# The second mixture's smallest expert in a round of 128 rows, with the rows as the stationary operand

## The chip, the core and the metric

The kernel runs on one core of a Trainium2 chip. Five engines work side by side, each with its own queue of instructions: TensorE (PE: products into PSUM banks; PEld is its loading of the stationary operand), VectorE (DVE), ScalarE (ACT), GpSimd (POOL) and SyncE (SP), which here issues the plain loads. The metric is the device time of one execution, in microseconds; lower is better.

## What is computed

A linear recurrence over 768 steps (its output is `x`, 3,072 tokens of 384 numbers), a first mixture of eight experts with 384 tokens each, and a second mixture, with which this case is concerned:

```python
def _moe2_ref(x, w_skip, w_gate, w1, w2):      # w1 [8, 384, 1024], w2 [8, 1024, 384]
    do_compute = x @ w_skip > 0
    out = x.copy()
    xc = x[do_compute]
    logits = xc @ w_gate
    e_idx = np.argmax(logits, axis=1)
    ...
    for e in range(E):
        mask = e_idx == e
        h = np.maximum(xc[mask] @ w1[e], 0.0)
        y[mask] = gate_w[mask, None] * (h @ w2[e])
    out[do_compute] = xc + y
```

How many tokens an expert of the second mixture gets follows from the data.

## The kernel before, in words

The kernel sorts the tokens of the second mixture by expert: each expert has 384 slots in a scratch tensor `xs2`, and the rows of its tokens are scattered there as the first mixture yields them. Slots without a token carry a row number out of bounds, so that the scatter of results passes over them.

The experts are taken by descending number of rows. `pick` finds the first, before the last tokens are known; its first 256 rows (`EARLY`) are computed while those arrive, and its next 128 (`LATE`) after. `ranks` sorts the other seven into rounds r = 1 to 7. The table `WIDE` says how many rows a round computes: 384 in round 1 and 256 in rounds 2 to 7 (entry 0 isn't used by the rounds). `ranks` also writes `room`, the number of rows that each expert's rounds cover; `rounds_more` compares it with the counts, and `moe2_more` runs further rounds over all experts if any count is larger. Whether it runs is told by `rest`, which every engine reads at the end, and SyncE already in the middle, ahead of the loads of round 1.

Products are made in three passes over float32 values split in two parts (`hi` and `lo`), which ScalarE (L976) and VectorE or POOL (L977) split from the loaded weights `raw`. Loads of weights have four `raw` buffers and the split ones twelve.

- `layer1` (L1018 on): for each of 8 blocks f of the hidden layer, 9 products `psh<-xT,hi` or `psh<-xT,lo` with the weights stationary and the rows moving, as many columns as the round has rows. ScalarE takes the relu (L1031), VectorE the difference (L1032).
- `layer1_few` (L1038 on), used so far for the first expert's 128 late rows: the rows are stationary and two blocks of weights (256 columns) move: `psh<-hi,xT`, 9 products for each of 4 groups. ScalarE takes the relu into `hr` (L1060), PE turns it (`pht<-ident,hr`, L112), ScalarE copies it (L1047) and VectorE makes the difference (L1048).
- `layer2` in `ffn2_out`: for each block of 128 rows, 8 x 3 products `psy<-...,hT` of 384 columns; then one output step on VectorE (`o<-psy`, L1223) and one scatter on POOL (L116).
- `prep2` issues the loads of the next round: the four weights of layer 1, the rows (`rows2`, L1174), the four of layer 2. `turn2` casts the row numbers (`ids`, L1202), turns the rows on PE (`pst<-ident,xg`, L112) and splits them (L985, L986).

`rows2` fills a tile with two buffers (`xg2`) for rounds of 256 rows or more, and a tile with one (`xl`) for 128. From the end of the first mixture on, a scheduler sets the order on each engine; loads wait in SyncE's queue until the buffer that they fill is free.

Of the kernel before, what the change touches and what calls it, by code (L numbers as in the profile page):

```python
# [8 lines left out]
F32 = mybir.dt.float32  # L9
# [5 lines left out]
ALU = mybir.AluOpType  # L15
# [16 lines left out]
def kernel_body(ctx, tc, q, k, v, a_re, a_im, w_gate, w1, w2, w_skip2, w_gate2, w12, w22, out):  # L32
    nc = tc.nc
    V = nc.vector
    B, H, S, D = q.shape
    DM = H * D
    E, _, F = w1.shape
# [5 lines left out]
    CAP = N // E  # L43


    ES = CAP
    WIDE = (CAP, CAP) + (256,) * (E - 2)
    MORE = 256

    EARLY, LATE = 256, 128  # L50
# [57 lines left out]
    def mat(*a, **kw):  # L108
        return pe(nc.tensor.matmul(*a, **kw))  # L109

    def tp(*a):
        return pe(nc.tensor.transpose(*a))  # L112
# [576 lines left out]
    room = rs.tile([128, E], F32, name="room")  # L689
# [5 lines left out]
    rw = ctx.enter_context(tc.tile_pool(name="rw", bufs=1))  # L695
# [322 lines left out]
    def layer1(w1h, xT, nt, tick=lambda: None, before=None, third=False):  # L1018
        hT = [fw.tile([128, KF, nt], F32R, tag=f"hT{i}", name="hT") for i in range(2)]
        for f in range(KF):  # L1020
            g, ff = divmod(f, FG)
            ps = pq.tile([128, nt], F32, tag="sm", name="psh") if third and f % 3 == 2 else pm.tile([128, nt], F32, tag="mm", name="psh")
            n = 0
            for a, b in PASSES:
                for c in range(KD):
                    mat(ps, lhsT=w1h[g][a][:, c, ff * 128:ff * 128 + 128], rhs=xT[b][:, c, :],
                       start=(n == 0), stop=(n == 3 * KD - 1))
                    n += 1
                    if n in (5, 9):
                        tick()  # L1030
            nc.scalar.activation(out=hT[0][:, f, :], in_=ps, func=ACTF.Relu)  # L1031
            V.scalar_tensor_tensor(out=hT[1][:, f, :], in0=ps, scalar=0.0, in1=hT[0][:, f, :].bitcast(F32),  # L1032
                                   op0=ALU.max, op1=ALU.subtract)
            if before:
                next(before, None)
        return hT

    def layer1_few(w1h, xT):  # L1038

        hT = [fw.tile([128, KF, 128], F32R, tag=f"hT{i}", name="hT") for i in range(2)]  # L1040

        def turned(g, h):
            pt = pt_.tile([128, FG, 128], F32, tag="t", name="pht")
            for f in range(FG):
                tp(pt[:, f, :], h[:, f * 128:(f + 1) * 128], ident)
            gs = slice(g * FG, (g + 1) * FG)
            nc.scalar.copy(out=hT[0][:, gs, :], in_=pt)  # L1047
            V.tensor_tensor(out=hT[1][:, gs, :], in0=pt, in1=hT[0][:, gs, :].bitcast(F32), op=ALU.subtract)  # L1048

        for g in range(NG):  # L1050
            ps = pm.tile([128, FG * 128], F32, tag="mm", name="psh")
            n = 0
            for a, b in PASSES:
                for c in range(KD):
                    mat(ps, lhsT=xT[b][:, c, :], rhs=w1h[g][a][:, c, :], start=(n == 0), stop=(n == 3 * KD - 1))
                    n += 1
            if g:
                turned(g - 1, h)
            h = rw.tile([128, FG * 128], F32, tag="R", name="hr", bufs=2)
            nc.scalar.activation(out=h, in_=ps, func=ACTF.Relu)  # L1060
        turned(NG - 1, h)
        return hT
# [48 lines left out]
    def route2(p, l2):  # L1111
# [37 lines left out]
        if p == E - 1:  # L1149
            ranks()  # L1150
# [16 lines left out]
    def by_load(r):  # L1167
        return ords[0:1, r:r + 1]

    def rows2(src, nj):  # L1170
        xg = fw.tile([128, nj, ROW], F32, tag="xg2", name="xg2", bufs=2) if nj > 1 else fw.tile([128, nj, ROW], F32, tag="xg", name="xl")

        def load_rows():
            nc.sync.dma_start(out=xg, in_=src)  # L1174
        return xg, load_rows

    def prep2(e, cap, shared, first=lambda: None):

        GF = FG * 128
        nj = cap // 128  # L1180
        if isinstance(e, int):
            er = slice(e, e + 1)
        else:
            er = nc.sync.value_load(e, min_val=0, max_val=E - 1)
            er = bass.ds(er, 1)
        xg, rows = rows2(xs2.rearrange("(e s) r -> e s r", e=E)[er, 0:cap, :].rearrange("o (j p) r -> p (o j) r", p=128), nj)
        w = weights(
            lambda g: w12[er, :, g * GF:(g + 1) * GF].rearrange("o (c p) f -> p (o c) f", p=128),
            lambda g: w22[er, g * GF:(g + 1) * GF, :].rearrange("o (c p) f -> p (o c) f", p=128), shared, {0: first, NG: rows})(2 * NG)
        return w, xg  # L1190

    def turn2(xg, res=None):
        res = [None] if res is None else res
        for _ in turn2_steps(xg, res):
            pass
        return res[0]
# [18 lines left out]
    def ffn2_out(xg, ids, w2h, hT, aside=True):  # L1215
        nj = xg.shape[1]
        pss = layer2(nj, 128, DM,
                     lambda f, a, b, j: hT[a][:, f, j * 128:(j + 1) * 128],
                     lambda f, a, b, j: w2h[f // FG][b][:, f % FG, :], aside=aside)
        o3 = fw.tile([128, nj, DM], F32, tag="yo", name="o3")  # L1220
        for j in range(nj):
            ot = o3[:, j, :]
            V.scalar_tensor_tensor(out=ot, in0=pss[j], scalar=xg[:, j, DM:DM + 1], in1=xg[:, j, 0:DM], op0=ALU.mult, op1=ALU.add)  # L1223
            scatter("out", out, ids[:, j:j + 1], ot, N - 1)
# [78 lines left out]
    def mixtures(exact, then=lambda: None):  # L1303
        (((w1h, w2h), xg), (ids, xT), last) = moe1(exact)
        hT = layer1(w1h, xT, EARLY, before=last)
        for _ in last:
            pass
        turn[1] = False
        res = then()
        er = nc.sync.value_load(head[0:1, 1:2], min_val=0, max_val=E * ES - LATE)  # L1310
        xl, load_rows = rows2(xs2[bass.ds(er, LATE), :].rearrange("(j p) r -> p j r", p=128), LATE // 128)
        nxt = prep2(by_load(1), WIDE[1], (2, 6), load_rows)
        ffn2_out(xg, ids, w2h, hT)
        ids, xT = turn2(xl)
        hT = layer1_few(w1h, xT)
        moe2_round(WIDE, by_load, 1, nxt, lambda: ffn2_out(xl, ids, w2h, hT))
        return res

    def moe2_round(caps, which, start=0, nxt=None, before=lambda: None):
        nxt = nxt or prep2(which(0), caps[0], (0, 1, 2))  # L1320
        cur = nxt + turn2(nxt[1])
        before()
        for r in range(start, E):
            (w1h, w2h), xg, ids, xT = cur
            hT = layer1(w1h, xT, caps[r], third=True)
            if r + 1 < E:
                nxt = prep2(which(r + 1), caps[r + 1], (2, 6))
                cur = nxt + turn2(nxt[1])
            ffn2_out(xg, ids, w2h, hT, aside=r + 1 < E)

    def ranks():

        sh = [128, E, E]
        kv = rw.tile([128, E], F32, tag="kv", name="kv")
        V.scalar_tensor_tensor(out=kv, in0=base2, scalar=float(E), in1=rev, op0=ALU.mult, op1=ALU.add)
        V.scalar_tensor_tensor(out=kv, in0=isfirst, scalar=FAR, in1=kv, op0=ALU.mult, op1=ALU.add)
        gt = rw.tile(sh, F32, tag="gt", name="gt")
        V.tensor_tensor(out=gt, in0=kv[:, None, :].to_broadcast(sh), in1=kv[:, :, None].to_broadcast(sh), op=ALU.is_gt)
        at_ = rw.tile([128, E], F32, tag="at_", name="at_")
        V.tensor_reduce(out=at_, in_=gt, axis=AX.X, op=ALU.add)  # L1340
        V.tensor_tensor(out=gt, in0=at_[:, None, :].to_broadcast(sh), in1=i128[:, 0:E, None].to_broadcast(sh), op=ALU.is_equal)
        V.tensor_tensor(out=gt, in0=gt, in1=rev[:, None, :].to_broadcast(sh), op=ALU.mult)
        V.tensor_reduce(out=kv, in_=gt, axis=AX.X, op=ALU.add)
        V.tensor_scalar(ords, kv, -1.0, float(E), op0=ALU.mult, op1=ALU.add)
        V.tensor_scalar(room, at_, float(WIDE.count(CAP)), float(CAP - MORE), op0=ALU.is_lt, op1=ALU.mult)
        V.tensor_scalar(room, room, float(MORE), None, op0=ALU.add)
        gap = rw.tile([128, E], F32, tag="gap", name="gap")
        V.tensor_scalar(gap, isfirst, float(EARLY), None, op0=ALU.mult)
        V.tensor_tensor(out=room, in0=room, in1=gap, op=ALU.subtract)
        V.scalar_tensor_tensor(out=room, in0=isfirst, scalar=ahead, in1=room, op0=ALU.mult, op1=ALU.add)  # L1350
# [99 lines left out]
```

## Time and profile before

| | us |
|---|---|
| median of 3 runs (lowest, highest) | 827.35 (827.09, 831.43) |
| the profiled execution | 826.72 |
| its span, first to last instruction | 824.8 |
| PE busy in the span | 705.2 (85%) |
| VectorE, ScalarE, POOL busy | 540.6, 389.0, 269.4 |
| mean granted clock of PE | 0.92 |

Times in the rows below count from the start of the span. "Idle before" an instruction, in square brackets, is followed by what ended it. A granted clock of 1.00 is full speed (2.4 GHz), 0.50 is 1.2 GHz. A busy time of PE includes the time in which products overlap, so the distance between the starts of two products is what one of them costs in a dense stretch.

### The profile page before, as it was taken

The numbers are of one execution on the slowest core, as the hardware profiler recorded it, in microseconds if no ns is written. First come the engines' busy times: TensorE is split into PE (matmuls) and PEld (weight loads), VectorE is DVE, ScalarE is ACT, GpSimd is POOL, SyncE is SP. The second block draws the span as 40 slices with busy tenths as digits, with TensorE's granted clock in tenths as the row PEclk, the third lists the DMA queues.
The fourth block names the chain that finished last, engine by engine and source line by source line (L and its number), as shares of the span: only waits on it lengthen the run. The fifth ranks groups of instructions, "written<-read, shape, count | busy, mean of one in ns | idle before, by whom it ended". The sixth has DMA issues, their size and how long they took to land.

```text
span 824.8 us, 14760 instructions
## 1 busy us (share of the span) xinstructions
PE 705.2 (85%) x5428; PEld 646.9 (78%) x5428; DVE 540.6 (66%) x1468; ACT 389.0 (47%) x682; POOL 269.4 (33%) x190
## 2 busy tenths in 40 slices
PE   1579879889999963888898898999999989999992
PEld 1468778788989952767787777898999979999992
DVE  8849789788756468789686787875534454544440
ACT  5775678667744313235151333343534255554530
POOL 1000545535501002010404041244214476776630
PEclk9669899999999975879997998999999989999996
DMA  9999565852411005144241515174206265566600
GB/s 171 175 293 164 76 129 108 131 110 64 72 41 40 20 31 181 45 138 147 65 136 53 177 37 175 33 228 135 72 16 201 87 212 192 193 210 227 226 27 12
DMA packets 183969, 100.03 MB, mean 121 GB/s; under 512 B 130963, under 2 KB 181129, under 8 KB 183888
## 3 DMA queue, kind: packets, MB, share of 16 engines
q1 hardware_dynamic: 178128, 86.99, 42.5%
q0 software_dynamic: 5760, 12.02, 4.3%
q8 instruction: 44, 0.72, 0.4%
q14 instruction: 37, 0.30, 0.1%
HBM read 82.23 MB, written 22.46 MB: 127 GB/s over the span
## 4 chain that ended last, share of the span: by engine, by line
PE 51%; DVE 18%; issue 9%; ACT 8%; DMA 8%; POOL 2%; SPq 2%; another core or an unknown queue 0%; DVEq 0%; POOLq 0%; ACTq 0%
PE psy L109 13%; PE psh L109 13%; DMA raw<-in_moe_w_dram 5%; PE py L109 4%; PE px L109 4%; PE pt L112 3%; DVE lo L977 3%; PE pa L109 3%; PE f L432 3%; PE st L109 2%; PE hist L109 2%; ACT hi L976 2%; DVE R L825 1%; DMA re<-in_a_re_dram 1%; DVE hT L1032 1%
## 5 line engine op out<-in xcount | busy, mean ns | idle before, releaser
L976 ACT CAST hi<-raw 128x768 fp32r<-128x768 f32 x128 | 107.0, 837 | 123.9 <-DMA raw<-in_moe_w_dram 92.0
L109 PE MATMUL psh<-xT,hi 128*128 128x384 f32 (+1 forms) x768 | 152.0, 330 | 6.9 <-DVE hT L1032 6.0
L109 PEld LDWEIGHTS psh<-xT,hi 128*128 128x128 f32 x768 | 124.1, 194 | 11.3 <-DVE hT L1032 8.3
L977 DVE TENSOR_TENSOR lo<-raw,hi 128x768 fp32r<-128x768 f32 x82 | 85.9, 1056 | 33.6 <-ACT hi L976 26.8
L109 PE MATMUL psy<-hT,hi 128*128 128x384 f32 x384 | 103.0, 350 | 0.0
L1031 ACT ACTIVATE hT<-psh 128x384 fp32r<-128x384 f32 (+1 forms) x128 | 56.0, 443 | 94.5 <-PE psh L109 89.0
L1032 DVE SCALAR_TENSOR_TENSOR hT<-psh,hT 128x384 fp32r<-128x384 f32 (+1 forms) x128 | 62.3, 492 | 53.6 <-ACT hT L1031 46.9
L977 POOL TENSOR_TENSOR lo<-raw,hi 128x768 fp32r<-128x768 f32 x46 | 85.4, 1875 | 33.5 <-ACT hi L976 22.8
L1002 POOL DMA_INDIRECT xg<-xd,ids x24 | 31.9, 1329 | 173.1 <-PE pp L109 62.4
L109 PE MATMUL psh<-xT,lo 128*128 128x384 f32 (+1 forms) x384 | 81.3, 321 | 0.0
L109 PE MATMUL psy<-hi,hT 128*128 128x384 f32 x288 | 79.3, 346 | 1.3 <-issue 1.3
L109 PEld LDWEIGHTS psy<-hT,hi 128*128 128x128 f32 x384 | 70.9, 194 | 0.6
L109 PE MATMUL psy<-hT,lo 128*128 128x384 f32 x192 | 68.9, 359 | 0.0
L109 PEld LDWEIGHTS psh<-xT,lo 128*128 128x128 f32 x384 | 65.3, 196 | 0.0
L109 PE MATMUL pa<-qT,kT 96*128 96x128 f32 x384 | 52.9, 284 | 1.7 <-ACT kT L497 1.7
L109 PEld LDWEIGHTS psy<-hi,hT 128*128 128x128 f32 x288 | 51.8, 192 | 1.8 <-issue 1.6
L116 POOL DMA_INDIRECT xs<-x,ix x24 | 25.0, 1043 | 80.2 <-issue 48.9
L109 PEld LDWEIGHTS pa<-qT,kT 96*128 96x128 f32 x384 | 49.2, 200 | 2.5 <-ACT kT L497 1.8
L985 ACT CAST xT<-pst 128x384 fp32r<-128x384 f32 (+1 forms) x49 | 19.5, 437 | 62.2 <-PE pst L112 62.2
L109 PE MATMUL psy<-lo,hT 128*128 128x384 f32 x144 | 48.7, 339 | 0.0
L109 PE MATMUL px<-iw,yT 128*128 128x104 f32 (+1 forms) x336 | 47.5, 288 | 0.6 <-ACT yT L548 0.6
L109 PEld LDWEIGHTS px<-iw,yT 128*128 128x128 f32 x336 | 42.8, 196 | 3.8 <-issue 2.7
(340 smaller groups left out, 1445.1 us busy)
## 6 DMA issues: line engine op xcount, KB each, us to landing
raw<-in_moe_w_dram SPq DMA_DIRECT2D x128, 384.0 KB
xs<-zt SPq DMA_DIRECT2D x8, 579.0 KB
re<-in_a_re_dram SPq DMA_DIRECT2D x24, 192.0 KB
im<-in_a_im_dram SPq DMA_DIRECT2D x24, 192.0 KB
q<-in_q_dram SPq DMA_DIRECT2D x24, 192.0 KB
k<-in_k_dram SPq DMA_DIRECT2D x24, 192.0 KB
vp<-in_v_dram SPq DMA_DIRECT2D x24, 192.0 KB
xd<-xo SPq DMA_DIRECT2D x24, 192.0 KB
```

The source lines that it names most:

```text
L109: return pe(nc.tensor.matmul(*a, **kw))
L112: return pe(nc.tensor.transpose(*a))
L116: st = nc.gpsimd.indirect_dma_start(out=dst, out_offset=bass.IndirectOffsetOnAxis(ap=idx, axis=0), in_=src, in_offset=None, bounds_check=b ...
L432: nc.tensor.matmul(f, lhsT=m, rhs=x, start=(j == 0), stop=(j == len(mm) - 1))
L825: V.scalar_tensor_tensor(out=R[:, sl], in0=PT[:, 0, sl, None].to_broadcast(shr), scalar=bp, in1=iot, op0=ALU.subtract, op1=ALU.is_ge)
L976: nc.scalar.copy(out=hi, in_=raw)
L977: st = (V if g in shared else nc.gpsimd).tensor_tensor(out=lo, in0=raw, in1=hi.bitcast(F32), op=ALU.subtract)
L985: nc.scalar.copy(out=xT[0][:, c, :], in_=ps)
L1002: st = nc.gpsimd.indirect_dma_start(out=xg[:, j, :], out_offset=None, in_=xd, in_offset=bass.IndirectOffsetOnAxis(ap=ids[:, j:j + 1], axis=0))
L1031: nc.scalar.activation(out=hT[0][:, f, :], in_=ps, func=ACTF.Relu)
L1032: V.scalar_tensor_tensor(out=hT[1][:, f, :], in0=ps, scalar=0.0, in1=hT[0][:, f, :].bitcast(F32), op0=ALU.max, op1=ALU.subtract)
```

## The change

Round 7 gets 128 rows instead of 256. It uses `layer1_few` instead of `layer1`, the one-buffer row tile, one block of layer 2 and one scatter. `ranks` writes 128 into `room` for the expert of rank 7 by two more VectorE steps.

```diff
-    WIDE = (CAP, CAP) + (256,) * (E - 2)
+    WIDE = (CAP, CAP) + (256,) * (E - 3) + (128,)
...
-            hT = layer1(w1h, xT, caps[r], third=True)
+            hT = layer1_few(w1h, xT) if caps[r] == 128 else layer1(w1h, xT, caps[r], third=True)
...
         V.tensor_scalar(room, room, float(MORE), None, op0=ALU.add)
+        few = rw.tile([128, E], F32, tag="few", name="few")
+        V.tensor_scalar(few, at_, float(E - 1), float(WIDE[-1] - MORE), op0=ALU.is_ge, op1=ALU.mult)
+        V.tensor_tensor(out=room, in0=room, in1=few, op=ALU.add)
```

On PE, the start of the last round of before, after the last product of round 6 (`psh` is layer 1, `psy` layer 2):

```order
L109 MATMUL psy<-hi,hT 128x384
L109 MATMUL psh<-xT,hi 128x256 x6
L109 MATMUL psh<-xT,lo 128x256 x3
L109 MATMUL psh<-xT,hi 128x256 x6
L109 MATMUL psh<-xT,lo 128x256 x3
L109 MATMUL psh<-xT,hi 128x256 x6
L109 MATMUL psh<-xT,lo 128x256 x3
L109 MATMUL psy<-hi,hT 128x384
```

The same place of the changed kernel, until the first group of layer 2 is through (`hr` is the relu's result, `pht` its turned form):

```order
L109 MATMUL psh<-lo,xT 128x256 x3
L112 MATMUL pht<-ident,hr 128x128 x2
L109 MATMUL psh<-hi,xT 128x256 x6
L109 MATMUL psh<-lo,xT 128x256 x3
L112 MATMUL pht<-ident,hr 128x128 x2
L109 MATMUL psh<-hi,xT 128x256 x6
L109 MATMUL psh<-lo,xT 128x256 x3
L109 MATMUL psy<-hi,hT 128x384
L109 MATMUL psy<-lo,hT 128x384
L109 MATMUL psy<-hi,hT 128x384 x2
L109 MATMUL psy<-lo,hT 128x384
L109 MATMUL psy<-hi,hT 128x384
```

The pair of transposes of one group stands behind the products of the next one; the third pair follows behind this piece, the fourth six products later.

On VectorE, from the end of round 5 on (`ids` are the row numbers of the last round, `o` the output steps of round 5), before:

```order
L986 TENSOR_TENSOR xT<-pst_9048,xT 128x256
L977 TENSOR_TENSOR lo<-raw,hi 128x768
L1223 SCALAR_TENSOR_TENSOR o_9103<-psy,xg_8749 128x384 x2
L1032 SCALAR_TENSOR_TENSOR hT<-psh,hT 128x256 x2
L1202 CAST ids_9269<-xg_9219 128x2
L1032 SCALAR_TENSOR_TENSOR hT<-psh,hT 128x256 x3
```

and in the changed kernel:

```order
L986 TENSOR_TENSOR xT<-pst_9051,xT 128x256
L1202 CAST ids_9272<-xl 128x1
L977 TENSOR_TENSOR lo<-raw,hi 128x768
L1223 SCALAR_TENSOR_TENSOR o_9106<-psy,xg_8752 128x384 x2
L1032 SCALAR_TENSOR_TENSOR hT<-psh,hT 128x256 x3
L986 TENSOR_TENSOR xT<-pst_9276,xT 128x384
```

The cast of the row numbers, which waits for their load, moved ahead of a weight difference and of the two output steps of round 5.

On VectorE in the middle, where `ranks` and `rounds_more` stand between steps of the first expert's early rows, the difference between before (-) and the changed kernel (+) is this, where only the line numbers changed in rows that stand in both:

```order
-L1350 SCALAR_TENSOR_TENSOR room<-isfirst,ahead,room 128x8
-L1355 TENSOR_TENSOR ov<-base_492,room 128x8
-L1357 TENSOR_REDUCE most<-ov 128x1
-L1359 TENSOR_SCALAR over<-lim,most 128x12
-L1032 SCALAR_TENSOR_TENSOR hT<-psh,hT 128x256
+L1352 TENSOR_TENSOR room<-room,gap 128x8
+L1353 SCALAR_TENSOR_TENSOR room<-isfirst,ahead,room 128x8
+L1358 TENSOR_TENSOR ov<-base_492,room 128x8
+L1360 TENSOR_REDUCE most<-ov 128x1
+L1032 SCALAR_TENSOR_TENSOR hT<-psh,hT 128x256
+L1362 TENSOR_SCALAR over<-lim,most 128x12
```

The difference of layer 1 (L1032) now runs ahead of `over`, on which `rest` depends.

## Rows read from the trace of the kernel before

**Rows 1.** Busy us (instructions) by stretch: PE, PEld, DVE, ACT, POOL; clock; DMA share, GB/s
```profile
660.00:680.00 20.00, 16.62 (x96) 15.73 (x95) 10.73 (x13) 10.38 (x21) 14.60 (x10) 0.83 0.69 216
...
792.00:805.00 13.00, 13.00 (x99) 13.00 (x99) 4.11 (x10) 3.07 (x8) 1.99 (x2) 1.00 0.05 20
...
810.00:825.00 15.00, 0.00 (x0) 0.00 (x0) 0.00 (x0) 0.00 (x0) 0.98 (x1) 0.58 0.04 14
```

**Rows 2.** Timeline of PE, last round: start, us, engine line, what, count
```profile
791.99 0.87 PE L109 MATMUL psh<-xT,hi 128*128 128x256 f32 x6
...
793.05 0.88 PE L109 MATMUL psh<-xT,hi 128*128 128x256 f32 x6
...
806.65 0.51 PE L109 MATMUL psy<-hi,hT 128*128 128x384 f32 x2
...
807.17 0.51 PE L109 MATMUL psy<-hi,hT 128*128 128x384 f32 x2
...
808.74 0.34 PE L109 MATMUL psy<-hi,hT 128*128 128x384 f32 x1
```

**Rows 3.** Timeline of PE, the first expert's 128 late rows
```profile
659.22 1.23 PE L109 MATMUL psh<-hi,xT 128*128 128x256 f32 x9
...
661.36 0.38 PE L112 MATMUL pht<-ident,hr 128*128 128x128 f32 x2
661.50 0.96 PE L109 MATMUL psh<-hi,xT 128*128 128x256 f32 x6
```

**Rows 4.** Timeline of PE, VectorE and ScalarE, the third group there
```profile
664.30 0.38 PE L112 MATMUL pht<-ident,hr 128*128 128x128 f32 x2
664.32 0.42 DVE L1048 TENSOR_TENSOR hT<-pht,hT 128x256 fp32r<-128x256 f32 x1 [0.34 <-ACT hi L976]
...
664.72 0.37 ACT L1047 CAST hT<-pht 128x256 fp32r<-128x256 f32 x1
```

**Rows 5.** Timeline of PE, round 6: its waits
```profile
780.86 0.97 PE L109 MATMUL psh<-xT,hi 128*128 128x256 f32 x6 [0.27 <-DVE hT L1032]
...
787.87 0.44 PE L112 MATMUL pst<-ident,xg 128*128 128x128 f32 x2 [0.32 <-DVE xT L986]
788.06 0.59 PE L109 MATMUL psy<-hi,hT 128*128 128x384 f32 x2
```

**Rows 6.** Timeline of VectorE and POOL at the end; DMA packets after 809 us
```profile
809.11 0.62 DVE L1223 SCALAR_TENSOR_TENSOR o<-psy,xg 128x384 f32<-128x384 f32 x1 [0.43 <-PE psy L109]
810.25 0.98 POOL L116 DMA_INDIRECT out_dram<-o,ids  x1 [0.30 <-issue]
...
q0 software_dynamic: 128, 0.17, 2.9%
```

**Rows 7.** Timeline of several engines and chain of waits, 651 to 671 us
```profile
651.04 0.42 DVE L1032 SCALAR_TENSOR_TENSOR hT<-psh,hT 128x256 fp32r<-128x256 f32 x1
...
659.06 5.88 DMA xg<-xs
...
664.53 5.39 POOL L977 TENSOR_TENSOR lo<-raw,hi 128x768 fp32r<-128x768 f32 x3
...
664.96 5.00 DVE L1202 CAST ids<-xg 128x3 int32<-128x3 f32 x1 [0.21 <-DMA xg<-xs]
...
670.34 0.90 PE L112 MATMUL pst<-ident,xg 128*128 128x128 f32 x3 [3.33 <-DVE hT L1048]
```

**Rows 8.** Timeline of SyncE, POOL and VectorE, 759 to 781 us
```profile
758.96 11.64 SPq L973 DMA_DIRECT2D raw<-in_moe_w_dram  x8
...
772.63 1.85 POOL L977 TENSOR_TENSOR lo<-raw,hi 128x768 fp32r<-128x768 f32 x1 [0.62 <-ACT hi L976]
...
775.58 1.14 DVE L1223 SCALAR_TENSOR_TENSOR o<-psy,xg 128x384 f32<-128x384 f32 x2
...
776.75 0.37 SPq L1174 DMA_DIRECT2D xg<-xs  x1
...
780.31 0.18 DVE L1202 CAST ids<-xg 128x2 int32<-128x2 f32 x1 [2.93 <-DMA xg<-xs]
```

## The prediction

> **What bounds the kernel now.** I read the busy time by stretches first, because the change touches one expert at the very end and an average over 824.8 us says nothing there. From 792 to 805 us TensorE (PE) is busy for 13.00 of 13.00 us at a granted clock of 1.00, that is 2.4 GHz, while the DMA share is 0.05: no weight is on its way any more, and nothing but the products sets the pace [rows 1]. After 810 us there is no product at all, 15 us in which one scatter (0.98 us of POOL) and the end of the program stand [rows 1]. So the end is: products of the last expert, its output, and a tail of fixed length.
>
> The timeline of PE gives the length of the last round (r = 7). It begins at 791.99 us and its last product ends at 808.74 + 0.34 = 809.08 us: 17.09 us [rows 2]. One f of layer 1 (6 + 3 products of 256 columns) takes 793.05 - 791.99 = 1.06 us, or 0.118 us a product; three products of layer 2 (384 columns) take 807.17 - 806.65 = 0.52 us, or 0.174 us each [rows 2]. The code issues 8 x 9 = 72 of the first kind and 8 x 2 x 3 = 48 of the second: 72 x 0.118 + 48 x 0.174 = 8.5 + 8.35 = 16.85 us, plus the drain of the last (0.34 - 0.174 = 0.17). That is the round; it holds no wait.
>
> **The last round, new form.** The same form runs once already, for the first expert's 128 late rows, so its prices are rows of this trace. The 18 products of its first two groups stand between 659.22 and the next instruction at 661.36: 2.14 us, 0.119 each [rows 3]. The turned form costs per product what the old one costs, but there are 4 x 9 = 36 instead of 72, since each covers two f at once. Added are 4 pairs of transposes; a pair takes 661.50 - 661.36 = 0.14 us of PE [rows 3]. Layer 2 has one block of 128 rows instead of two, 24 products. Sum: 36 x 0.119 + 4 x 0.14 + 24 x 0.174 + 0.17 = 4.28 + 0.56 + 4.18 + 0.17 = 9.19 us against 17.09: **-7.9 us**. All of it lies on PE, which sets the end.
>
> What hides the new steps: each group's result goes PE, ScalarE (relu), PE (transposes), ScalarE (copy, 0.37), VectorE (difference, 0.42), PE. In the first expert's round the copy starts 664.72 - 664.30 = 0.42 us after the transposes start, so copy and difference are there 0.42 + 0.37 + 0.42, with hand-overs about 1.3 us, after them [rows 4]. In the new order six products of layer 2 (6 x 0.174 = 1.04) and the pair (0.14) stand between a pair and the first product that needs it, and that product needs only the copy (0.8 us after the pair); the difference is needed two products later, at 1.18 + 0.35 = 1.5. So 1.3 us fit under 1.5, by 0.2. ScalarE and VectorE have no weights to split any more by then. I take **+0.2** for it; without that cover all four groups would wait about 1 us once, at the end, so the ends are 0 and +1.0.
>
> **The round before it (r = 6).** It carries the next expert's transposes. Now 6 become 3, and one PSUM tile instead of three takes them. Before, the third pair waits 0.32 us for a tile and takes 788.06 - 787.87 = 0.19, and a product waits 0.27 us at 780.86 for a VectorE step that stood behind the row numbers' cast [rows 5, 8]. Two pairs more at 0.14 [rows 3]. Together 0.51 + 0.27 + 0.28 = 1.06 us, less three transposes at 0.07 = 0.2: **-0.8 us**, ends -1.1 and +0.5 (the upper one is for the new order on ScalarE, where the cast of the first layer-2 weights moves ahead of the relu of the second f; that load can start only when a weight buffer comes free, and lands about 3.5 us later, as the row load from 776.75 to 780.31 did [rows 8]).
>
> **The loads.** The last rows' load on the SyncE queue is at 776.75 us because the two-buffer tile it fills is still read by an output step at 775.58 to 776.72; the changed kernel uses the one-buffer tile of the first expert, free since long ago [rows 8]. So this load and the four weight loads behind it go out some 5 us earlier. Worth nothing here, since PE waits for no weight in the last round [rows 1].
>
> **The tail.** Before, two output steps and two scatters: the second output step ends at 809.11 + 0.62 = 809.73, the second scatter starts at 810.25, held 0.30 behind the first [rows 6]. One scatter alone starts up to 0.5 us sooner after its output. Against this: after 809 us the scatters moved 0.17 MB [rows 6], 109 rows of 1,536 bytes; so the first one carried all and the second none, while now the only one carries the rows and its data land later after its start. From 810.25 to 824.8 are 14.55 us; I take them unchanged plus **+0.3**, ends -0.5 and +1.0.
>
> **The table of rooms, in the middle.** Two small VectorE steps of 128x8 are added, and the step `over` now stands behind the difference that ran at 651.04 for 0.42 us [rows 7]. I put `rest`, which follows, 0.5 us later. SyncE waits for it ahead of the loads of the second expert's rows and weights, and those rows landed 5.88 us after 659.06 [rows 7]. Who waits: VectorE's cast of the row numbers at 664.96, which then took 5.00 us while three POOL steps ran (664.53, 5.39 us), and behind it the step for which PE stood 3.33 us, until 670.34 [rows 7]. If POOL's steps keep their time the delay vanishes in that stand; if they shift with the weights it comes through whole. Ends 0 and +0.6, **+0.4** taken, because POOL's steps wait for the same queue.
>
> **Sum.** -7.9 + 0.2 - 0.8 + 0.3 + 0.4 = -7.8 us. The profiled execution took 826.72 us (span 824.8 and 1.92 around it): 818.9 us. The median of the runs, 827.35, lies 0.6 above the profiled one, which I keep as part of the range.
>
> **Rivals.** *A cast that blocks VectorE* (part of the gain lost). In the new order the cast of the last rows' numbers stands ahead of the weight difference and of both output steps of round 5. It waits for the load, which I put at 774.5 (the queue is through with the weight loads ahead of it at 758.96 + 11.64 = 770.6, plus some 0.4 to issue and 3.5), and POOL runs a weight step from 772.63 to 774.48 [rows 8]. The same cast took 0.18 us with POOL idle and 5.00 us beside POOL [rows 7, 8]. If it is held for one such step, 1.85 us, the output steps and with them PE's PSUM banks come as much later: 820.8 us; held as long as in the middle, 823.8. Against it: POOL's queue has a pause just then, and the cast has one column, not three. 0.12. The Trainium skill, page "SBUF — State Buffer", section "SBUF: two separate sides", says VectorE and GpSimd share a port pair as an exclusive lock, held for a whole instruction, while the loser fully blocks. By that rule the loss would be at most one POOL step; the 5.00 us of this trace lasted through three.
>
> *Cold last round* (slower). After the 3.33 us stand PE ran on at a lower clock; the stretch 660 to 680 us has a granted clock of 0.83 [rows 1, 7], full and half speed (2.4 and 1.2 GHz) in turn. If the chain through ScalarE and VectorE, or the cast, left PE idle as long as that just ahead of the last round, and the clock stayed at half for all of it, 9.0 us of work would take 9.0 more, with 3.3 of idle: 818.9 + 12.3 = 831.2 us. [...] 0.04.
>
> *The room is too small* (the change does not do what it says). If the least expert had 129 rows or more, the loop for rows left over would run: 8 rounds of 17.1 us [rows 2] and 24 scatters of 1.28 us [rows 6], some 168 us more, 987 us. The 0.17 MB say 109 rows [rows 6]. 0.01.
>
> **How the numbers follow.** The forecast has 0.83 and is the likeliest: 818.9 us. Its own range is the sum of the ends: -7.9 + 0 - 1.1 - 0.5 + 0 = -9.5, or 817.2, and -7.9 + 1.0 + 0.5 + 1.0 + 0.6 = -4.8, or 821.9. The 0.6 between profile and median would widen it upwards, and the first rival's 820.8 lies inside; I give 817.0 to 822.0. About what a measurement of this kernel can tell is 0.5%, 4.1 us: faster means under 823.2. All of the forecast and nearly all of the first rival are there: 0.92 faster; the tail of that rival and part of the second 0.05 within; 0.03 slower.
>
> **What the profile of the changed kernel would show.** Right: the last round on PE some 9.2 us long, from its first product of 256 columns with the rows stationary to its end near 801 us; no wait over 0.3 us in it; one output step and one scatter after it, and about 14.5 to 15.5 us from the scatter's start to the end; round 6 without its two waits. Wrong: idle time on PE ahead of the four transposes' users, a cast of the row numbers of over a microsecond in round 6, a granted clock under 1.00 after 780 us, or a span from last product to the end that grew by over 1 us (then the tail was not fixed). A stand at 666 us of another length than 3.33 would show the middle mis-sized.

## The result, and the profile after

| | before | after |
|---|---|---|
| median, us (20 runs each) | 825.39 | 817.37 |
| the profiled execution, us | 826.72 | 818.81 |
| its span, us | 824.8 | 817.0 |
| PE busy, us | 705.2 | 696.1 |
| VectorE, ScalarE, POOL busy, us | 540.6, 389.0, 269.4 | 537.9, 389.1, 267.5 |

The ratio of the times is 0.9906, 95% interval 0.9883 to 0.9929: faster by 0.7 to 1.2%. Medians are of all executions; ratios, means and their intervals, here and below, leave out those more than 1.5% above the fastest of the same kernel. The profiled execution is 7.91 us shorter.

Where the time went is read stretch by stretch, as [rows 1] were: busy us and instructions of PE, PEld, VectorE, ScalarE and POOL, then the granted clock, the DMA share and GB/s, here of the changed kernel.

```profile
660.00:680.00 20.00, 17.44 (x111) 16.57 (x111) 11.61 (x15) 11.60 (x22) 13.92 (x9) 0.94 0.79 246
780.00:792.00 12.00, 12.00 (x83) 12.00 (x82) 6.81 (x7) 3.95 (x8) 7.42 (x5) 1.00 0.18 53
792.00:802.00 10.00, 9.33 (x68) 8.94 (x66) 3.10 (x7) 2.81 (x8) 1.99 (x2) 1.00 0.07 27
802.00:817.00 15.00, 0.00 (x0) 0.00 (x0) 0.00 (x0) 0.00 (x0) 0.98 (x1) 0.62 0.06 16
```

PE still sets the end: busy for all of 780 to 792 at full clock and on to 801.3, then 15 us without a product. The last round, on the timeline of PE (start, us, engine, line, what, count):

```profile
791.79 0.87 PE L109 MATMUL psh<-hi,xT 128*128 128x256 f32 x6
...
793.93 0.38 PE L112 MATMUL pht<-ident,hr 128*128 128x128 f32 x2
794.07 0.96 PE L109 MATMUL psh<-hi,xT 128*128 128x256 f32 x6
...
796.52 0.34 PE L109 MATMUL psy<-hi,hT 128*128 128x384 f32 x1
...
797.58 0.38 PE L112 MATMUL pht<-ident,hr 128*128 128x128 f32 x2
797.71 0.42 PE L109 MATMUL psy<-hi,hT 128*128 128x384 f32 x1
797.97 0.34 PE L109 MATMUL psy<-lo,hT 128*128 128x384 f32 x1
...
800.99 0.34 PE L109 MATMUL psy<-hi,hT 128*128 128x384 f32 x1
```

It runs from 791.79 to 800.99 + 0.34 = 801.33: 9.54 us for 17.09 [rows 2], and no row of it shows a wait. The first 18 products take 793.93 - 791.79 = 2.14 us, as in [rows 3]. What was not priced is behind the pairs of transposes: the pair takes 0.13 us, but the product after it takes 797.97 - 797.71 = 0.26 us instead of 0.174. With the 0.14 of [rows 3] a pair costs 0.14 + 0.09 = 0.23 us, and the sum becomes 36 x 0.119 + 4 x 0.23 + 24 x 0.174 + 0.17 = 9.55 us.

The third group there, with ScalarE's copy and VectorE's difference (what ended their idle time in brackets), answers [rows 4]:

```profile
797.99 0.37 ACT L1047 CAST hT<-pht 128x256 fp32r<-128x256 f32 x1 [0.83 <-PE pht L112]
798.40 0.42 DVE L1048 TENSOR_TENSOR hT<-pht,hT 128x256 fp32r<-128x256 f32 x1 [1.80 <-ACT hT L1047]
```

The copy starts 797.99 - 797.58 = 0.41 us after the transposes, the difference is through at 798.82, 1.24 us after them: it fits.

Round 6 lasts 18.20 us (773.59 to 791.79), before 18.67. The waits of [rows 5] are gone and two others came. SyncE, VectorE and PE there:

```profile
771.07 0.35 SPq L1174 DMA_DIRECT2D xl<-xs  x1
...
776.18 0.15 DVE L1202 CAST ids<-xl 128x1 int32<-128x1 f32 x1 [2.53 <-DMA xl<-xs]
776.29 0.96 DVE L977 TENSOR_TENSOR lo<-raw,hi 128x768 fp32r<-128x768 f32 x1
777.16 1.14 DVE L1223 SCALAR_TENSOR_TENSOR o<-psy,xg 128x384 f32<-128x384 f32 x2
...
777.32 0.34 PE L109 MATMUL psy<-lo,hT 128*128 128x384 f32 x1
777.83 0.44 PE L109 MATMUL psy<-hi,hT 128*128 128x384 f32 x1 [0.17 <-DVE o L1223]
778.11 0.34 PE L109 MATMUL psy<-lo,hT 128*128 128x384 f32 x1
...
778.68 0.98 PE L109 MATMUL psh<-xT,hi 128*128 128x256 f32 x6 [0.23 <-DVE hT L1032]
```

The load of the last rows is issued 5.7 us earlier than in [rows 8], as expected. But its data are there 5.1 us later, before 3.6. The cast behind it stands on VectorE until then, 776.2 us, and the output steps of round 5 behind the cast come at 777.16 instead of 775.58.

PE waits 0.17 and 0.23 us for that, and pays more. The number in brackets counts from the end of the product before, and in a dense stretch the next product has begun before that end. From start to start, 777.32 to 777.83 and 778.11 to 778.68 are 0.51 and 0.57 us for one product each, where a dense stretch has 0.174. What follows each wait takes another 0.1 us more than in a dense stretch. The two waits cost some 0.95 us.

The DMA engines differ too. While the changed kernel's load is on its way they are full; in the kernel before they are idle when it is issued (the changed kernel first):

```profile
771.00:774.00 3.00, 3.00 (x20) 3.00 (x20) 0.42 (x1) 1.91 (x3) 2.27 (x2) 1.00 1.09 351
...
776.00:777.00 1.00, 1.00 (x9) 1.00 (x9) 1.00 (x4) 0.52 (x2) 0.52 (x1) 1.00 0.00 0
```

The DMA share is 1.09 in the first and 0.00 in the second. The same holds in the other traces where VectorE or ScalarE waits for this load (256 rows in the kernel before, 128 in the changed one): issued with a share of 0.75 to 0.98 in the microsecond ahead of it, it took 4.95 to 5.91 us (five traces, this one among them); with a share of 0.00, 2.61 to 3.78 (four).

The tail, which answers [rows 6]: from PE's end to the span's end 15.67 us, before 15.72; from the last scatter's start 14.73, before 14.55. The one scatter moved the 0.17 MB that two did.

```profile
801.37 0.62 DVE L1223 SCALAR_TENSOR_TENSOR o<-psy,xl 128x384 f32<-128x384 f32 x1 [1.28 <-PE psy L109]
802.27 0.98 POOL L116 DMA_INDIRECT out_dram<-o,ids  x1 [7.43 <-DVE o L1223]
...
q0 software_dynamic: 64, 0.17, 3.4%
```

The middle, which answers [rows 7]. L1147 is the last counting step ahead of `ranks`:

```profile
648.33 0.18 DVE L1147 TENSOR_TENSOR rk<-pp,base 128x24 f32<-128x24 f32 x1 [1.98 <-PE pp L109]
...
653.57 0.15 DVE L1409 TENSOR_TENSOR rest<-left,nov 1x1 int32<-1x1 f32 x1
...
667.47 5.41 POOL L977 TENSOR_TENSOR lo<-raw,hi 128x768 fp32r<-128x768 f32 x3
...
668.45 4.47 DVE L1202 CAST ids<-xg 128x3 int32<-128x3 f32 x1
...
673.29 0.55 PE L112 MATMUL pst<-ident,xg 128*128 128x128 f32 x3 [2.51 <-DVE hT L1048]
```

From L1147 to `rest` are 5.39 us, before 5.12. PE's stand is 2.51 us instead of 3.33, and from L1147 to the start of round 6 are 125.26 us instead of 126.72; most of that difference is PE's clock (last section). L1147 itself starts 1.73 us later, after the same program in both. The sum: -7.55 (last round) - 0.47 (round 6) - 0.05 (tail) - 1.46 (middle) + 1.73 (ahead of L1147) = -7.80 us of span, and -0.11 outside of it.

### The profile page after: what moved, and what is told of

Read it like the earlier page. It is cut to its first block, busy times and chain, and to the rows that moved or that the text cites. A ratio compares the mean times of both kernels' runs of the same rounds, so it can differ in the third digit from the quotient of the medians.

```text
span 817.0 us, 14643 instructions
## 1 busy us (share of the span) xinstructions
PE 696.1 (85%) x5373; PEld 638.9 (78%) x5373; DVE 537.9 (66%) x1463; ACT 389.1 (48%) x680; POOL 267.5 (33%) x189
## 4 chain that ended last, share of the span: by engine, by line
PE 53%; DVE 19%; DMA 8%; ACT 7%; issue 6%; SPq 4%; POOL 2%; another core or an unknown queue 0%; DVEq 0%; POOLq 0%; ACTq 0%
PE psh L109 15%; PE psy L109 14%; DMA raw<-in_moe_w_dram 5%; PE py L109 4%; DVE lo L977 4%; PE px L109 4%; PE f L432 3%; PE pt L112 3%; PE pa L109 3%; SPq L332 3%; PE st L109 2%; PE hist L109 2%; ACT hi L976 2%; DVE hT L1032 1%; DVE R L825 1%
## 5 line engine op out<-in xcount | busy, mean ns | idle before, releaser
L109 PE MATMUL psh<-xT,hi 128*128 128x384 f32 (+1 forms) x720 | 144.4, 332 | 8.4 <-DVE hT L1032 6.3
L109 PEld LDWEIGHTS psh<-xT,hi 128*128 128x128 f32 x720 | 117.6, 195 | 12.6 <-DVE hT L1032 8.8
L1031 ACT ACTIVATE hT<-psh 128x384 fp32r<-128x384 f32 (+1 forms) x120 | 52.8, 446 | 82.5 <-PE psh L109 72.4
L1032 DVE SCALAR_TENSOR_TENSOR hT<-psh,hT 128x384 fp32r<-128x384 f32 (+1 forms) x120 | 59.0, 499 | 48.3 <-ACT hT L1031 41.1
L109 PE MATMUL psy<-hi,hT 128*128 128x384 f32 x272 | 75.5, 347 | 2.4 <-issue 2.0
L109 PE MATMUL psh<-xT,lo 128*128 128x384 f32 (+1 forms) x360 | 76.9, 323 | 0.0
L109 PEld LDWEIGHTS psh<-xT,lo 128*128 128x128 f32 x360 | 61.9, 197 | 0.0
L109 PEld LDWEIGHTS psy<-hi,hT 128*128 128x128 f32 x272 | 49.0, 192 | 3.2 <-issue 2.3
L109 PE MATMUL psy<-lo,hT 128*128 128x384 f32 x136 | 46.1, 339 | 0.0
```

## The experiments

The time of one execution scatters: the lowest and the highest of 20 are some 2% apart. So what is told apart here by less than 1% is told by the trace first, and by times only with their interval. Each kernel's ratio is to the kernel before, run beside it.

**The rows moving.** Round 7 keeps its 128 rows, but the weights are stationary, as in the other rounds.

```diff
-            hT = layer1_few(w1h, xT) if caps[r] == 128 else layer1(w1h, xT, caps[r], third=True)
+            hT = layer1(w1h, xT, caps[r], third=True)
```

> The changed kernel with one part undone: the last round still has 128 rows, but layer 1 has the weights stationary and the 128 rows moving (72 products of 128 columns, no transposes of the hidden layer). If a product costs what its columns cost, the nearest row is the transposes of 128 columns, 0.07 us each: 72 x 0.07 = 5.0 us, and 24 products of layer 2 at 0.174 plus 0.17 of drain give a last round of 9.4 us against 9.54 in the changed kernel: no difference in time, and the stationary rows were not needed. If a product cannot be shorter than the 0.118 us that it costs with 256 columns, because the load of its stationary operand takes as long, layer 1 takes 8.5 us and the round 12.85, so 3.3 us more than the changed kernel and 4.5 us (0.5%) less than the kernel before. I hold the second for nearer, at about 0.09 to 0.118 each: a round of 10.8 to 12.9 us. The Trainium skill, page "TensorE: Matmul & The Clock Gate", section "Back-to-back issue gap", gives 81 ns a product at 128 columns in a stream of loads and products; by that the round would be 10.2 us.

Measured: the last round took 793.99 to 806.40 = 12.41 us, 2.9 more than with the rows stationary. The timeline of PE:

```profile
793.99 0.78 PE L109 MATMUL psh<-xT,hi 128*128 128x128 f32 x6
794.61 0.50 PE L109 MATMUL psh<-xT,lo 128*128 128x128 f32 x3
794.95 0.83 PE L109 MATMUL psh<-xT,hi 128*128 128x128 f32 x6
```

The round is inside the 10.8 to 12.9 us expected. Nine products of 128 columns take 794.95 - 793.99 = 0.96 us, 0.107 each, not the 0.07 of the transposes, and more than the 0.081 that the expectation sets beside it: half the columns of the old form save a tenth of the time. So of the 7.55 us of the last round 4.7 come from the halved row count and then 2.9 from making the rows stationary. The time, 815.25 us, 0.9909 (0.9868 to 0.9949), could not tell the 2.9 us from the changed kernel's 0.9906.

**256 rows stationary.** The kernel before, its last round with two blocks of 128 rows stationary, each with its transposes (`layer1_few` takes the number of blocks).

```diff
-            hT = layer1(w1h, xT, caps[r], third=True)
+            hT = layer1_few(w1h, xT, 2) if r == E - 1 and start else layer1(w1h, xT, caps[r], third=True)
```

> The kernel before with the other part alone: the last round keeps its 256 rows, but they are the stationary operand, in two blocks (72 products of 256 columns, 8 pairs of transposes). If PE sets the end and the gain came from half the rows, this is a loss: 72 x 0.1236 + 8 x 0.14 + 8 x 0.09 for the hand-over behind each pair + 48 x 0.174 + 0.17 = 19.3 us against 17.09, 2.2 us slower than the kernel before (0.3%). If the stationary rows themselves brought the gain, it would be faster than the kernel before by up to 3 us. It has no change in the table of rooms, so the middle stretch should be that of the kernel before: PE stands for about 3.3 us ahead of the first transposes of round 1.

Measured: a last round of 788.72 to 807.65 = 18.93 us, 1.84 longer than before's; 823.02 us, 1.0026 (0.9988 to 1.0064). A row of it, the last pair:

```profile
805.14 0.38 PE L112 MATMUL pht<-ident,hr 128*128 128x128 f32 x2
805.28 0.43 PE L109 MATMUL psy<-hi,hT 128*128 128x384 f32 x1
805.54 0.34 PE L109 MATMUL psy<-lo,hT 128*128 128x384 f32 x1
```

Again 0.14 and 0.26. With 0.23 a pair: 72 x 0.119 + 8 x 0.23 + 48 x 0.174 + 0.17 = 18.93; in the 19.3 expected, the 0.1236 a product held part of the 0.09 already. The turned form has nothing to give at 256 rows, where it only adds transposes; its gain exists at 128.

**The table alone.** The two new steps of `ranks` on the kernel before, adding zero.

```diff
+        few = rw.tile([128, E], F32, tag="few", name="few")
+        V.tensor_scalar(few, at_, float(E - 1), 0.0, op0=ALU.is_ge, op1=ALU.mult)
+        V.tensor_tensor(out=room, in0=room, in1=few, op=ALU.add)
```

> The kernel before with the two VectorE steps of the table alone (they add zero). The prediction's price: rest is ready some 0.5 us later and the time is longer by 0.4 us, 0.05%, which no comparison of times can show; the trace should show the time from the last L1147 step to rest longer by 0.3 to 0.6 us (4.97 us before), and PE's stand ahead of the first transposes of round 1 still there, 2.5 to 3.5 us. The rival: the two steps shorten that stand and so keep the clock up; then the stretch from that step to the first product of round 6 is about 1.5 us shorter than the 126.7 us of the kernel before, as it was in the changed kernel. If it is neither, the stretch varies from execution to execution.

Measured: L1147 to `rest` 5.38 us, 0.26 more; L1147 to round 6 126.04, 0.7 less than before; 821.12 us, 1.0007 (0.9979 to 1.0035). The stand is still there, 2.91 us, and no cost of the table is seen behind it.

**The two-buffer tile.** The changed kernel with the last rows in `xg2`, so that their load again waits for the output step of round 5 (`prep2` passes `deep`).

```diff
-        xg = fw.tile([128, nj, ROW], F32, tag="xg2", name="xg2", bufs=2) if nj > 1 else fw.tile([128, nj, ROW], F32, tag="xg", name="xl")
+        xg = fw.tile([128, nj, ROW], F32, tag="xg2", name="xg2", bufs=2) if nj > 1 or deep else fw.tile([128, nj, ROW], F32, tag="xg", name="xl")
```

> The changed kernel, but the last round's 128 rows are loaded into the two-buffer tile that the other rounds use, so that their load waits again for an output step, as before, and the cast of the row numbers stands behind the output steps of round 5. If the two new waits at the start of round 6 (0.17 and 0.23 us) come from the cast that stood ahead of the output steps and waited for its load until 776.18 us, they are gone, and round 6 takes 17.8 us instead of 18.2, unless the old wait of 0.27 us in its middle comes back (then 18.1). The last round stays at 9.5 us. If the waits have another cause, round 6 keeps them. In the time, under 0.1% against the changed kernel; 0.990 of the kernel before.

Measured: round 6 takes 768.09 to 786.16 = 18.07 us. VectorE and then PE:

```profile
770.11 1.13 DVE L1223 SCALAR_TENSOR_TENSOR o<-psy,xg 128x384 f32<-128x384 f32 x2
...
773.88 0.15 DVE L1202 CAST ids<-xg 128x1 int32<-128x1 f32 x1 [1.63 <-DMA xg<-xs]
...
779.77 0.98 PE L109 MATMUL psh<-xT,hi 128*128 128x256 f32 x6 [0.23 <-DVE hT L1032]
```

The output steps are no longer behind the cast, and the two early waits went with it; another of 0.23 us came later. So the cast that stood ahead of the output steps made the two waits. Round 6 as a whole gained 0.13 us by the tile. 814.28 us, 0.986 (0.975 to 0.997, from four times).

**The cast, three ways.** In the five traces so far with the cast of the second expert's row numbers beside three POOL steps it took 4.5 to 5.0 us, with a stand of PE of 2.5 to 3.3 us behind it. The changed kernel was run again as a measure:

> The changed kernel itself once more, as the measure for the three runs beside it. If the 0.9906 of its first comparison is the change and not the hour: 0.988 to 0.993 of the kernel before, a last round of 9.5 us, a stand of 2.5 to 3.3 us ahead of the turning of the second expert's rows. The stretch from the last step at L1147 to the start of round 6 was 126.7, 125.3, 125.5, 126.7, 126.8 and 126.0 us in the six executions so far; if that is chance of the execution, it falls in 125 to 127 here too, and the changed kernel's 125.3 was no gain of the change.

Measured: 813.11 us, 0.9932 (0.989 to 0.9973); last round 9.54, stand 2.91, L1147 to round 6 127.17. The 127.17 lies just outside of the 125 to 127 expected. So the 125.26 of the first trace was that execution, not the change.

Beside it the cast behind the hidden layer's last difference, where no step that PE waits for stands behind it (each cast waits for `done1[0]`, the last difference):

```diff
-        V.tensor_copy(ids, xg[:, :, DM + 1])
...
+        st = V.tensor_copy(ids, xg[:, :, DM + 1])
+        tc.add_manual_dep(st.ins, done1[0].name, order, reason="the hidden layer first")
```

> The changed kernel with each cast of row numbers put behind the hidden layer's last difference on VectorE instead of as soon as the rows land. First theory: in the middle the cast, held 4.5 to 5.0 us beside three POOL steps, is what TensorE stands 2.5 to 3.3 us for, through the difference behind it. Then the stand ahead of the second expert's transposes falls under 1 us, L1147 to round 6 gets some 2 to 4 us shorter (121.5 to 124.5), and the kernel takes 0.985 to 0.988 of the kernel before instead of 0.9906. In round 6 the two waits of 0.2 us go as well, since the cast of the last rows then stands ahead of nothing. Second theory: the rows' landing or another VectorE step beside POOL holds TensorE as long; then a stand of over 2 us stays at the same place with another step named, and the time is that of the changed kernel within 0.3%.

and the cast on ScalarE:

```diff
-        V.tensor_copy(ids, xg[:, :, DM + 1])
+        nc.scalar.copy(out=ids, in_=xg[:, :, DM + 1])
```

> The changed kernel with the cast of the row numbers on ScalarE, at the same places of the program. First theory, that VectorE and POOL hold each other: on ScalarE the cast of 128x3 beside the same three POOL steps takes 0.2 to 0.5 us, the stand ahead of the second expert's transposes falls under 1 us, and the time is 0.985 to 0.988 of before. Second theory, that the numbers' tile or their load is what makes the cast long: then it takes over 3 us on ScalarE too, ScalarE's copies behind it come late and the stand stays. The price against it: while ScalarE waits for the rows, the relu's copies and weight casts behind it wait too, as VectorE's did, some tenths of a microsecond.

Late, the cast is still held beside POOL, but nobody waits; VectorE and POOL of that kernel:

```profile
686.30 1.79 DVE L1217 CAST ids<-xg 128x3 int32<-128x3 f32 x1
...
684.42 5.46 POOL L977 TENSOR_TENSOR lo<-raw,hi 128x768 fp32r<-128x768 f32 x3 [1.61 <-ACT hi L976]
```

On ScalarE it takes 0.19 us beside POOL steps; POOL, ScalarE and PE of that kernel:

```profile
658.74 7.41 POOL L977 TENSOR_TENSOR lo<-raw,hi 128x768 fp32r<-128x768 f32 x4
...
660.13 0.19 ACT L1202 CAST ids<-xg 128x3 int32<-128x3 f32 x1
...
662.49 0.49 PE L112 MATMUL pst<-ident,xg 128*128 128x128 f32 x3
...
767.60 0.44 PE L109 MATMUL psy<-hi,hT 128*128 128x384 f32 x1 [0.71 <-ACT hT L1031]
```

In both, the stand is gone (the row at 662.49 has no wait), and L1147 to round 6 is 122.08 and 120.91 us. The last row is the price foreseen for ScalarE: it waits for the last rows in round 6, and PE 0.71 us for a relu behind. Round 6 took 17.26 us with the late cast, without any wait, and 18.45 with ScalarE's. The first theory holds in the traces: with the stand went 2.91 us, and some 1.5 us that half the clock had cost behind it (0.50 for 3 us in the trace beside, 1.00 in these two). The times were 812.53 us, 0.9932 (0.9879 to 0.9984), and 810.84 us, 0.9916 (0.9871 to 0.9962): the 5 to 6 us by which these two traces are shorter than the one beside them are not found in the times.

The late cast with the two-buffer tile:

> The late cast and the two-buffer tile for the last rows together, as a version that might beat both kernels. If the two gains are separate and each is what it was alone, the time is that of the late cast alone less 0 to 0.4 us: 0.984 to 0.988 of before. With the cast no longer ahead of the output steps of round 5, the tile has nothing left to give: equal to the late cast alone within 0.3%.

Measured: 811.04 us, 0.9922 (0.9888 to 0.9955), 121.11 us from L1147 to round 6. Against the late cast alone nothing can be told.

**Whether the gain is real.** Three more on one chip: the late cast on the kernel before, the changed kernel, and the version with both edits.

> The kernel before with the late cast of row numbers alone. In the traces of the changed kernel with the late cast, with the cast on ScalarE and with both edits, the way from the last step at L1147 to the end of the span was 164.1 to 164.6 us against 168.7 and 170.5 of the changed kernel, that is 4.1 to 6.4 less, but their times were only 1.9 us lower together (0.1 to 3.7). First theory, the gain is real and separate from the change, and the times of twelve runs scatter: here from L1147 to the end 172.5 to 174.5 us instead of before's 178.2, no stand over 1 us ahead of the second expert's transposes, and 0.993 to 0.997 of before. Second theory, most of the gain in those traces was the luck of single executions: L1147 to the end 176 to 178 us, 0.997 to 1.001 of before.

> The changed kernel once more beside the two others: another execution's trace from L1147 to the end (168.7 and 170.5 us so far; if single executions differ by as much as the gain in question, it falls outside of 167 to 172), and twelve more times. 0.988 to 0.994 of before.

> The late cast and the two-buffer tile on the changed kernel once more. First theory: 163 to 166 us from L1147 to the end, and 3 to 5 us under the changed kernel beside it over the two sets of runs together. Second theory: 166 to 169 us, and within 2 us of the changed kernel.

| | median, us | ratio to before | L1147 to the end, us |
|---|---|---|---|
| before, late cast | 825.02 | 1.0000 (0.9956 to 1.0044) | 172.5 |
| changed | 816.74 | 0.9927 (0.9889 to 0.9966) | 167.1 |
| changed, late cast, two-buffer tile | 813.73 | 0.9873 (0.9835 to 0.9911) | 167.3 |

Neither theory came out whole. The changed kernel's 167.1 us lie at the edge of the 167 to 172 expected; its three traces have 168.7, 170.5 and 167.1. The third shows why a single one says little: its cast was not held that time, and PE stood elsewhere. PE, POOL and VectorE of it:

```profile
656.16 0.44 PE L109 MATMUL psy<-hi,hT 128*128 128x384 f32 x1 [2.72 <-ACT hT L1031]
...
664.50 7.35 POOL L977 TENSOR_TENSOR lo<-raw,hi 128x768 fp32r<-128x768 f32 x4
...
665.71 0.73 DVE L1202 CAST ids<-xg 128x3 int32<-128x3 f32 x1
```

The cast began inside the first of four POOL steps and was through just after the second could begin (664.50 + 7.35 / 4 = 666.34 us; the cast ended at 666.44). PE's stand of 2.72 us elsewhere had half the clock behind it too, from 657.5 to 660.9 us. In seven of the eight traces with the cast on VectorE as soon as the rows land, the cast or `lo` (last section) was held and PE stood 2.5 to 3.3 us; in this one not. So the gain from taking the cast away differs from execution to execution. By the means of the times, the version with both edits lies 2.2 us under the changed kernel in the first set and 3.5 in the second, together 2.9 us (1.2 to 4.5): a version that beats both, by less than half a percent. On the kernel before the trace gave 172.5 us as the first theory said (178.2 for the kernel before as it was), yet the mean time is only 1.0 us less, give or take 2.8: whether the late cast helps there stays open.

## Why the prediction was right, point by point

The forecast, 818.9 us and -7.8, met 818.81 of the profiled execution and 817.37 of the median, inside of 817.0 to 822.0. The main term was right by its mechanism: less work on PE, which sets the end, at prices read from the trace. That the sum fits to a tenth is luck; the other terms missed by more and cancelled.

- **Last round**: -7.7 with its allowance of +0.2, measured -7.55. Prices of products and the cover were right. The last round took 9.54 and 9.55 us in two more executions of the changed kernel. The +0.2 was put on a chain that would come late; the trace has no such wait, and the 0.35 us above 9.19 are the first product after each of four pairs. The allowance was right by luck. [rows 3] had the 0.09 already: six products behind the pair are busy 0.96 us there, six without one 0.87 [rows 2].
- **Round 6**: -0.8, measured -0.47. The old waits and two pairs went, and that was worth more than was said: without any wait the round takes 17.26 us (late cast), 1.41 less than before. The waits had been priced by their numbers in brackets, and the product behind each pair was left out. The two new waits took 0.94 of it back, 18.20 for 17.26. The step that failed here is the landing of the last rows, put at 774.5 us: the load was issued at 771.07, as worked out, but landed 5.1 us later, not 3.6 as in [rows 8], where the 3.6 was measured on idle DMA engines and the earlier load found them full. That this is the cause is argued from the traces alone; no run changed only it. So VectorE stood at the cast ahead of the output steps; with the two-buffer tile those two waits were gone.
- **Loads**: 0. The earlier load won nothing and, with the cast where it was, caused the above.
- **Tail**: +0.3, measured -0.05; from the scatter on it grew by 0.18, and 0.23 came back ahead of it.
- **Table**: `rest` 0.5 later, measured 0.27, and 0.26 with the table alone, which cost the kernel nothing that can be seen. The term of +0.4 was too large. In its place the first trace shows -1.46 for the middle, and +1.73 ahead of it: neither is of the change, since the changed kernel's own middle took 127.17 us in another execution and the start of L1147 lay between 639.0 and 650.0 us over the traces with the same program ahead of it. That these two cancel made the sum look exact.
- **A cast that blocks VectorE**: its place was right, its mechanism was not. VectorE stood for the load; the cast itself took 0.15 us. (The 0.18 us of [rows 8] were not measured with POOL idle: a scatter ran on POOL from 779.50 to 780.50 us.) The page "SBUF — State Buffer" of the Trainium skill, section "SBUF: two separate sides", was weighed there on its exclusive lock, held for a whole instruction. In the middle both are seen: a wait until the next POOL step could begin (0.73 us), and waits through all three (4.47 us here, 5.00 in [rows 7]), which is more than one step.
- **Cold last round**: the granted clock was 1.00 from 780 us on, so no; from 680 us on PE was never idle for 0.3 us.
- **The room is too small**: no further round ran; a smaller room was not tried. (0.17 MB, as rounded, are 107 to 113 rows of 1,536 bytes; the 109 cannot be read from it.)

## What to carry to other kernels

Price a new form by a place where the trace already has it, down to the product behind an added step, since that is where the 0.09 us a pair were. Price a wait from the start of one product to the start of the next, not by the idle time alone: 0.17 and 0.23 us of idle cost 0.95 here. Before making a buffer free earlier, ask which queue the consumer of that load stands in: an early wait in an in-order queue holds whatever is behind it. And ask what else the DMA engines carry at the earlier time: the load that took 3.6 us when issued on idle engines took 5.1 on full ones. Where single executions differ by more than the effect, take the verdict of a term from the length of its own stretch, and look whether the same stretch repeats in a second execution.

## What the runs showed of the hardware

- VectorE's steps with a source in PSUM (L1032, L1048) kept 0.4 us beside POOL's weight steps (0.42 at 668.11 in the changed kernel's trace, where POOL ran from 667.47 to 672.88); the cast could be held, and so could the weight difference `lo`, whose operands all lie in SBUF. In the trace of the 256 stationary rows, where the cast came while POOL paused and took 0.15 us, it was `lo` that was held, and PE stood 3.12 us behind that instead:

```profile
661.93 4.82 DVE L977 TENSOR_TENSOR lo<-raw,hi 128x768 fp32r<-128x768 f32 x1 [3.33 <-ACT hi L976]
...
667.23 0.41 PE L112 MATMUL pht<-ident,hr 128*128 128x128 f32 x2 [3.12 <-DVE hT L1048]
```

The page "SBUF — State Buffer" of the Trainium skill, section "SBUF: two separate sides", names steps with two inputs in SBUF among those that wait for POOL; this row agrees, with 4.82 us for a step that takes 0.96 elsewhere.

- The granted clock was at half behind some stands of PE and at full behind others, and their length alone does not say which. In the kernel before, PE ran at 0.50 from 670.3 to 675.8 us, behind the stand of 3.33 us [rows 1, 7]. In the changed kernel it was 0.50 from 658.9 to 662.3, behind a stand of 2.01 us, and 1.00 behind the 2.51 us that end at 673.29, so the 0.94 of the row from 660 to 680 is not of that stand. In the trace of the 256 stationary rows it was 1.00 behind 3.12 us (667.23). The changed kernel, then that trace:

```profile
658.90 0.69 PE L109 MATMUL psy<-hi,hT 128*128 128x384 f32 x1 [2.01 <-issue]
...
659.00:662.00 3.00, 3.00 (x11) 2.90 (x12) 0.79 (x3) 0.52 (x2) 0.00 (x0) 0.50 0.90 274
673.00:680.00 7.00, 6.66 (x40) 6.28 (x41) 3.54 (x7) 4.46 (x8) 4.66 (x3) 1.00 0.60 183
...
667.00:680.00 13.00, 12.72 (x77) 12.29 (x78) 5.37 (x13) 8.10 (x15) 9.76 (x6) 1.00 0.69 223
```

PE ran at half the clock for 5.5 us before and for 3.4 in the changed kernel, which makes some 1.05 of the 1.46 us by which the middle was shorter. With the late cast it was 1.00 in the whole of that stretch:

```profile
660.00:680.00 20.00, 19.40 (x117) 18.70 (x116) 7.89 (x14) 11.62 (x21) 18.20 (x11) 1.00 0.74 234
```

- A product of 128 columns in a dense stretch cost 0.107 us, one of 256 columns 0.118, one of 384 columns 0.174.
